# Turning the attention output by DMA during the forward chain instead of in the FFN phase and the gradient phase

## The chip, the core and the metric

The kernel runs on one core of a Trainium2 chip. The metric is the device time of one execution in microseconds (us); the time before is the median of three runs. Matmuls run on TensorE (PE, with its weight loads on PEld), copies out of PSUM and elementwise work on VectorE (DVE) and ScalarE (ACT), some copies on GpSimd (POOL). DMAs are issued from two places: SyncE's queue (SP; plain copies and transposing copies) and POOL's queue (plain copies). Both kinds are carried out by the same 16 DMA engines.

## The reference, cut to what matters

A forward pass and its gradient for one layer: pre-LN attention with a recurrent memory, then a SwiGLU FFN. 2048 tokens of width 448, 16 heads of 256 (so the concatenated heads O have 4096 columns), 64 segments of 32 tokens with 8 memory tokens each.

```python
for s in range(n_seg):                       # 64 segments, each needs the memory of the one before
    h = concat([mem, xs])                    # 8 + 32 tokens
    q, k, v = h @ Wq, h @ Wk, h @ Wv         # 16 heads of 256
    p = softmax(mask(q @ k.T * scale))
    o = (p @ v) @ Wo                         # p @ v is O, 4096 columns
    mem = o[:, :M]; outs.append(o[:, M:])
h = x + attention(layernorm(x)); out = h + (silu(g) * u) @ w_down   # g, u from layernorm(h)
# and the gradients of x, mem0, Wq, Wk, Wv, Wo, w_gate, w_up, w_down
```

The gradient of Wo is the product of O, transposed, with the gradient of the attention's output, summed over all tokens. For that, O is needed with tokens on the partitions. The forward chain leaves it with columns on the partitions.

## The kernel before, in words

The order of all work is written by hand; each engine works through its own list in that order. There are four stages.

**Forward chain** (`forward_chain`, the loop from L785): 64 steps `s`, four to a tile of 128 tokens (`t, r = divmod(s, 4)`). A step projects K, Q and V (L818 to L844, matmuls L558 and L566), transposes K and Q (L572), computes the scores (L603), the softmax (L851 to L867), the transposed probabilities (L876), O (L910, in four groups: half 0 and half 1, each for two groups of heads), and O times Wo (L687), whose sum over partitions (L611, L616) is the memory that the next step starts with. Beside that, each step carries a quarter of the work on the memory rows of the neighbouring tile (`cur`, `late`, `late2`).

The V rows that L910 reads stand in one buffer, `V_sb` (one copy). It is filled from two sides. Rows 32 to 39 of each group of heads, the last tokens of the segment, come by four small DMAs from SP at the start of a step (`v_b_rows`, L751); the buffer must have been read by the step before, and at r = 0 the copy that the rows come from must have been made. The other rows come from `Vev` by `v_shift`: some by POOL, DVE and ACT copies, and three by DMAs from SP (`D_`, L755): half 0 of groups 2 and 3 as soon as ACT has copied the first half of V out of PSUM, half 1 of group 0 after the second half. L910's first group needs neither of the first two; the second needs them; the third needs the last one.

SP's list in a step is, in this order: `v_b_rows` (4 DMAs, L751), `v_shift` (3 DMAs, L755), the stores of K and Q (L858, L859), two stores of `V_sb` (L894), at r = 0 a load of the next tile's rows (L536), at r = 2 a store of the finished rows (L741). POOL's list: two small copies (L807, L808), two `v_shift` copies (L524), the store of the probabilities (L891), a small copy (L950), at two of four steps a store of K or Q of the next tile's last tokens (L663), and at r = 3 the stores of the tile's O: `OTA` (1 MB, L959) and `OTB` (256 KB, L960).

**FFN phase** (`ffn_phase`, the loop from L1256): 14 iterations `i` and an end written out. Iteration `i` runs the gate and up products of one tile, the gradients of the tile before, and stores z, the two FFN gradients and the gradient of h from POOL. A transposing DMA on SP turns z (L1280). After that, from i = 3 to i = 13, `o_turn(3)` (L1281, L1215) takes the next three pieces of O, from a list `quarters` of columns 0 to 2047 of all tiles: a transposing DMA from `OTA` to one of three buffers in the weights' region (L1220, SP, [128 x 1024] in eight blocks), and a store from there to `OTok` (L1221, POOL). In the last iteration and after it, Wv, Wk and Wq are loaded transposed for the backward chain, each in two pieces (`load_back`, L1034, SP), as the FFN weights that they overwrite are used up: the first half of Wv follows the last gate product (L1105). In between SP issues the first loads for the backward chain (L1501, L1503, L1511). The end's stores go through POOL: L1171, L1174, L1192, L1195.

**Backward chain** (`backward_chain`): 64 steps, last to first. The change does not touch it.

**Gradient phase** (`tail_phase`): 22 phases; phase `p` multiplies one loaded operand X of [128 x 16 or 20 tiles x 1024], and issues the load for phase p + 2 (`load_phase`). Phases 6 to 21 are the four quarters of the gradients of Wv, Wk, Wq and Wo, in the order of the list `seg`. A quarter is loaded turned, by 16 transposing DMAs on SP, one for each tile (`seg_x`, L1828), or plainly from `OTok`, by two DMAs (`seg_o`, L1836). Before the change the quarters 0 and 1 of Wo are loaded plainly and 2 and 3 turned.

The tiles of a stage lie at fixed places of one arena; the strings `FWD`, `FFN`, `BWD` and `TAIL` (L94 to L117) list names, sizes and places in bytes.

Of the kernel before, what the change touches and what calls it, by code (L numbers as in the profile page):

```python
# [10 lines left out]
BF16 = mybir.dt.bfloat16  # L11
# [4 lines left out]
P = 128  # L16
# [77 lines left out]
FWD = """oA#0:8192 oB#0:2048 bev:2048x2  # L94
kB#0:2048 qB#0:2048 bevv#0:2048 kB#1:2048 qB#1:2048 bevv#1:2048 PT0:1280 PT1:1280 P_sb0:1024 hB#0:256
xload:1024 aT#0:1024
kT:2560 qT:2560 Kev:2048 Qev:2048 E_sb:1280
@43264 oA#1:8192 oB#1:2048
@54016 V_sb:4096 hA:2048
@61184 part:2048 partB:2048 Vev:2048 aT#1:1024  # L100
xtmp:1024x2 x2load:1024x2 P_sb1:1024 S_sb:640x2 maskr:640 maskf:160 hB#1:256"""
FFN = """WdT:14336
h_ld:896x3 hn:1024x3 dout_ld#2:1024x2 dh_t:1792 lnb_prod:1792 lnb_t1:1792 dh_b:896 o_t:896x2
@30464 dout_ld#0:1024x2
# [389 lines left out]
def forward_chain(k: _K, hA, NWIN, Wq_sb, Wk_sb, Wv_sb, Wo_sb, maskr, work, stage, ff, feed):  # L494
    nc, tc = k.nc, k.tc
    S, D, M, H, Dh, HD = k.S, k.D, k.M, k.H, k.Dh, k.HD
    SEG, L, NSEG, NT, KC, DP, MC, DC = k.SEG, k.L, k.NSEG, k.NT, k.KC, k.DP, k.MC, k.DC
    X2 = k.aps["A_x"][0]
    ident, identf, dr = k.ident, k.identf, k.dr
# [254 lines left out]
    def D_(out, in_):  # L754
        nc.sync.dma_start(out=out, in_=in_)  # L755

    def v_shift(V_sb, Vev, half, gs, eng):
        for g in gs:
            gg, g2 = divmod(g, 2)
            o = V_sb[QB * gg:QB * gg + SEG, g2 * GF + half * HB:g2 * GF + (half + 1) * HB]  # L760
            eng(o, Vev[32 * g:32 * g + 32, half * HB:(half + 1) * HB])
# [23 lines left out]
    for s in range(NSEG):  # L785
        t, r = divmod(s, 4)
# [18 lines left out]
        kT = work.tile([P, MC, L], BF16, name="kT", bufs=1)  # L805
        qT = work.tile([P, MC, L], BF16, name="qT", bufs=1)
# [8 lines left out]
        Kev = work.tile([P, GF], BF16, name="Kev", bufs=1)  # L815
        Qev = work.tile([P, GF], BF16, name="Qev", bufs=1)
# [29 lines left out]
        mx, ssum, rs, S_sb = [], [], [], []  # L846
        E_sb = work.tile([P, 2, HQ, L], FP32, name="E_sb", bufs=1)
# [30 lines left out]
        def p_ev(half, e, eng):  # L878
            eng(PT[QB * e:QB * e + L, half, :, e * L:(e + 1) * L].rearrange("p (g a) n -> p g a n", g=2),
                ppt[half][QB * e:QB * e + L, 0:2 * P].rearrange("p (a g n) -> p g a n", a=2, g=2)[:, :, :, 0:L])  # L880
# [8 lines left out]
        p_ev(1, 0, V)  # L889
        p_ev(1, 1, V)  # L890
        nc.gpsimd.dma_start(out=dr["P_all"][s], in_=P_sb[0:NR].rearrange("p h n -> p (h n)"))  # L891

        for gg in range(2):
            nc.sync.dma_start(out=dr["Vtok"][s, gg], in_=V_sb[QB * gg:QB * gg + 48, :])  # L894
        if s == NSEG - 3:
            next(feed)

# [29 lines left out]
        for i in range(MC):  # L927
            c = order[i]
# [95 lines left out]
def load_back(k, v, src, head, c0=0, c1=None):  # L1024
    nc = k.nc
    D, HD = k.D, k.HD
    if head:
        full = D // P
        for kc in range(full):
            nc.sync.dma_start_transpose(out=v[:, kc, :], in_=src[:, kc * P:(kc + 1) * P])  # L1030
        nc.sync.dma_start_transpose(out=v[:, full, :], in_=src[:, D - P:D])
        nc.gpsimd.memset(v[0:P - (D - full * P), full, :], 0.0)
    else:
        nc.sync.dma_start_transpose(out=v[:, c0:c1, :], in_=src[:, c0 * P:c1 * P])  # L1034


def ffn_phase(k: _K, WT, ff, work, mv2, rstd2, srcs, back):
    nc, tc = k.nc, k.tc
    S, D, F = k.S, k.D, k.F
    NT, KC, DP, FC = k.NT, k.KC, k.DP, k.FC  # L1040
    ps1, ident, dr = k.ps1, k.ident, k.dr
# [24 lines left out]
    def load(t):  # L1066
        o = T[t]
        o.h = work.tile([P, D], BF16, name="h_ld", bufs=3)
        nc.sync.dma_start(out=o.h[:], in_=dr["Hh"][rows(t), :])
        o.dout = work.tile([P, DP], BF16, name="dout_ld", bufs=4)  # L1070
        nc.sync.dma_start(out=o.dout[:, 0:D], in_=GO2[rows(t), :])
        nc.sync.dma_start(out=o.dout[:, D:DP], in_=GO2[rows(t), D - rem:D])
# [65 lines left out]
    def turn_f(src, dst, engs):  # L1138
        for half in range(2):
            pzb = ps1(BF16)  # L1140
            for j in range(FH):
                c = half * FH + j
                nc.tensor.transpose(pzb[:, j * P:(j + 1) * P], src[:, c * P:(c + 1) * P], ident[:, :])
            engs[half](dst[:, half * FH:(half + 1) * FH, :], pzb[:, 0:FH * P].rearrange("p (c n) -> p c n", n=P))

    def dz(t):
        o = T[t]
        o.dz = work.tile([P, F], BF16, name="dz", bufs=1)
        for pair in range(NB // 2):
            for b, pz in enumerate(mm_d(o.doutT, ff.WdT, pair)):  # L1150
                f = slice((2 * pair + b) * BW, (2 * pair + b + 1) * BW)
                A(o.dz[:, f], pz[:, 0:BW])

    def down_mm(t):
        T[t].pf = k.fix[0]
        for c in range(FC):
            nc.tensor.matmul(T[t].pf[:, 0:D], lhsT=ff.zT[:, c, :], rhs=ff.Wd[:, c, :], start=(c == 0), stop=(c == FC - 1))
# [30 lines left out]
    def dh_ln(t):  # L1188
        o = T[t]
        dh_t = work.tile([P, D], FP32, name="dh_t", bufs=1)  # L1190
        k.ln_bwd(dh_t[:], k.fix[1][:, 0:D], o.hn[:, 0:D], rstd2[:, t:t + 1], o.dout[:, 0:D], work, smal, D)
        nc.gpsimd.dma_start(out=dr["DH"][rows(t), :], in_=dh_t[:])  # L1192
        o.dhb = work.tile([P, D], BF16, name="dh_b", bufs=1)
        V(o.dhb[:], dh_t[:])
        nc.gpsimd.dma_start(out=dr["DHb"][rows(t), :], in_=o.dhb[:])  # L1195
# [14 lines left out]
        A(dT[:], pt[:, 0:KC * P])  # L1210
        nc.gpsimd.dma_start(out=dr["doutT"][t], in_=dT[:])

    quarters = [(t, q) for t in range(NT) for q in range(2)]

    def o_turn(n):  # L1215
        for t, q in quarters[:n]:
            b = ff.ot[len(quarters) % 3]
            del quarters[0]
            cols = slice(q * 1024, (q + 1) * 1024)
            nc.sync.dma_start_transpose(out=b.rearrange("n (c p) -> n c p", p=P), in_=dr["OTA"][t][:, cols])  # L1220
            nc.gpsimd.dma_start(out=dr["OTok"][t][:, cols], in_=b)  # L1221
# [34 lines left out]
    for i in range(NT - 2):  # L1256
        t, n1, n2 = ORD[i:i + 3]
        if i > 0:
            load(n2)
        if i == 2:  # L1260
            load_back(k, WT["o"], srcs["o"], True)
        if i == NT - 6:
            next(back)
        if not 1 < i < NT - 2:
            turn_f(T[t].z, ff.zT, (A, A))
        dz(t)
        if i > 0:
            dh_ln(t - 1)
        down_mm(t)
        if i == 0:  # L1270
            rstd(NT - 1, NT)
        grads(t)
        if i > 0:
            dh_out(t - 1)
        gate(n1)
        down_ev(t)
        norm(n2)
        up(n1)
        if 0 < i < NT - 3:
            nc.sync.dma_start_transpose(out=ff.zT, in_=T[n1].z)  # L1280
        if 2 < i < NT - 2:  # L1281
            o_turn(3)
        if i == NT - 3:
            dout_turn(n1)
            hn_turn(n2)
            gate(n2)
            load_back(k, WT["v"], srcs["v"], False, 0, HC)
            up(n2)
            load_back(k, WT["v"], srcs["v"], False, HC, 2 * HC)
            dh_turn(t)  # L1290
            slope(n1)
            slope(n2)
        else:
            dh_turn(t)
            dout_turn(n1)
            hn_turn(n2)
            slope(n1)
        dh_mm(t)
    p, q = ORD[NT - 2:]
# [483 lines left out]
def tail_phase(k: _K, work):  # L1783
    nc, tc = k.nc, k.tc
    S, D, M, HD, F = k.S, k.D, k.M, k.HD, k.F
    SEG, NSEG, NT, KC, MC = k.SEG, k.NSEG, k.NT, k.KC, k.MC
    ps1, ident, identf, dr = k.ps1, k.ident, k.identf, k.dr
# [37 lines left out]
    def seg_x(srcA, q, p):  # L1825
        X = k.Wall[:, k.xpos[p] * 512:k.xpos[p] * 512 + NKT * 1024].rearrange("p (t f) -> p t f", t=NKT)
        for t in range(NT):
            nc.sync.dma_start_transpose(out=X[:, t, :].rearrange("n (c p) -> n c p", p=P),  # L1828
                                        in_=srcA[t][:, q * 1024:(q + 1) * 1024])
        return X  # L1830

    def seg_o(q, p):
        X = k.Wall[:, k.xpos[p] * 512:k.xpos[p] * 512 + NKT * 1024].rearrange("p (t f) -> p t f", t=NKT)
        v = dr["OTok"].rearrange("t n f -> n t f")[:, :, q * 1024:(q + 1) * 1024]
        for a in range(0, NT, NT // 2):
            nc.sync.dma_start(out=X[:, a:a + NT // 2, :], in_=v[:, a:a + NT // 2, :])  # L1836
        return X
# [124 lines left out]
    Xs = {}  # L1962
    lds = {}
    lns = {}
    turned = [(w, q) for w in "vkq" for q in range(NQ)]
    seg = turned[0:3] + [("o", 0)] + turned[3:7] + [("o", 1)] + turned[7:12] + [("o", 2), ("o", 3)]
    assert NQ == 4
    srcA = {"v": dr["dVA"], "k": dr["dKA"], "q": dr["dQA"], "o": dr["OTA"]}
    srcB = {"v": dr["dVB"], "k": dr["dKB"], "q": dr["dQB"], "o": dr["OTB"]}
# [5 lines left out]
    def load_phase(p):  # L1975
        if p >= NP:
            return
        if p == 0:
            Xs[p] = (k.z_low, z_high)
        elif p < 6:  # L1980
            Xs[p] = k.ffn_half(ffn[p], p, 1)
        else:
            w, q = seg[p - 6]
            Xs[p] = seg_o(q, p) if w == "o" and q < 2 else seg_x(srcA[w], q, p)

    z_high = work.tile([P, NT // 2, F // 2], BF16, name="z_high", tag="h1")
    nc.sync.dma_start(out=z_high, in_=k.z_high)
# [6 lines left out]
    for p in range(NP):  # L1994
# [23 lines left out]
        if 5 <= p < NP - 1:  # L2018
            if p not in lds:
                w, q = seg[p - 5]  # L2020
# [14 lines left out]
        else:  # L2035
            w, q = seg[p - 6]
# [45 lines left out]
```

## Time and profile before

| | us |
|---|---|
| median of three runs | 2923.17 (2922.85 to 2923.99) |
| the profiled execution, its own time | 2936.97 |
| its span | 2935.2 |
| PE busy | 2722.7 (93% of the span) |
| DVE busy | 1561.3 |
| ACT busy | 1082.5 |
| POOL busy | 762.1 |
| from 60 to 950 us (forward chain): PE busy, DMA share | 847.10 of 890, 0.42 |
| from 2300 to 2910 us (gradient phase): PE busy, DMA share | 608.10 of 610, 1.04 |

The DMA share is the mean busy share of the 16 DMA engines; packets of two queues that overlap count twice, so it can pass 1. Time to landing of a DMA is shown for POOL's DMAs only. What is drawn for SP's DMAs is the time that SP takes to issue them, not the transfer. A releaser named "issue" is a wait for which the profile shows nothing.

### The profile page before, as it was taken

To read this page: it belongs to the slowest core of one execution; us is meant where nothing else is said; L and a number is where in the kernel's file an instruction comes from. 1 tells how busy PE (TensorE), PEld (TensorE's weight loads), DVE (VectorE), ACT (ScalarE), POOL (GpSimd) and SP (SyncE) were. 2 spreads that over 40 slices of the span, in tenths; PEclk is the share of its full clock that TensorE was granted. 3 is DMA by queue.
4 is the path that set the end of the run, shared out by engine and by line. 5 is a ranking of instruction groups with operands and counts; after the bars stand their busy time and mean duration, and the time that the engine had idled before them with its cause. 6 is when DMAs were issued, how large, how long until landed. Compare 5 with 4: busy or idle time off the path is not lost.

```text
span 2935.2 us, 104407 instructions
## 1 busy us (share of the span) xinstructions
PE 2722.7 (93%) x44384; PEld 1514.8 (52%) x44420; DVE 1561.3 (53%) x4196; ACT 1082.5 (37%) x2880; POOL 762.1 (26%) x1420
## 2 busy tenths in 40 slices
PE   3999999999998799987999999999999999999999
PEld 1555555555554455543555555555555454545454
DVE  4666666666665578874666666666665112222221
ACT  2444444444443455552444444434433111111110
POOL 2222222222222223321222222222222222233222
PEclk7999999999999899998999999999999999999999
DMA  9334434343435899997655655565556999999992
GB/s 273 116 123 134 126 123 137 116 130 122 135 116 140 217 218 233 245 226 166 151 156 153 189 152 161 155 175 152 161 151 215 334 228 227 209 225 241 204 224 69
DMA packets 652001, 515.86 MB, mean 176 GB/s; under 512 B 508592, under 2 KB 558112, under 8 KB 642000
## 3 DMA queue, kind: packets, MB, share of 16 engines
q1 hardware_dynamic: 600640, 309.09, 47.5%
q0 software_dynamic: 50896, 200.09, 20.5%
q8 instruction: 350, 5.73, 0.8%
q14 instruction: 115, 0.94, 0.1%
HBM read 145.89 MB, written 230.33 MB: 128 GB/s over the span
## 4 chain that ended last, share of the span: by engine, by line
PE 69%; DVE 15%; DMA 7%; issue 5%; SPq 2%; ACT 2%; POOL 1%; DVEq 0%; ACTq 0%; POOLq 0%
PE psf L1919 13%; PE psf L558 9%; PE psf L1392 9%; DVE arena L1355 5%; PE psf L687 4%; PE psf L1880 4%; PE psf L1105 3%; PE psf L1701 3%; PE psf L566 3%; PE psf L1364 2%; PE psh L572 2%; PE psf L1932 2%; PE psf L910 2%; PE psf L1399 2%; DMA wall<-in_A_Wv_dram 2%
## 5 line engine op out<-in xcount | busy, mean ns | idle before, releaser
L1919 PE MATMUL psf<-wall,arena 128*128 128x512 bf16 (+1 forms) x1788 | 390.6, 373 | 1.9
L521 ACT CAST arena<-psf 128x512 bf16<-128x512 f32 (+2 forms) x560 | 235.8, 453 | 362.4 <-PE psf L558 251.3
L1392 PE MATMUL psf<-wall,arena 128*32 128x448 bf16 x6144 | 336.8, 361 | 17.0 <-DMA wall<-in_A_Wq_dram 11.9
L1358 ACT CAST arena<-psf 128x256 bf16<-128x256 f32 (+1 forms) x597 | 233.0, 417 | 304.2 <-PE psf L1364 214.0
L558 PE MATMUL psf<-wall,arena 112*32 112x512 bf16 x5120 | 308.9, 384 | 31.0 <-DMA wall<-in_A_Wk_dram 14.0
L1919 PEld LDWEIGHTS <-arena 128*128 128x128 bf16 x1824 | 176.2, 98 | 198.3 <-issue 4.7
L1807 DVE CAST arena<-psf 128x448 bf16<-128x448 f32 (+1 forms) x83 | 54.7, 659 | 418.7 <-PE psf L1919 267.1
L518 DVE CAST arena<-psf 128x512 bf16<-128x512 f32 (+2 forms) x432 | 191.8, 469 | 123.7 <-PE psf L558 83.8
L1392 PEld LDWEIGHTS <-arena 128*32 128x32 bf16 x6144 | 154.9, 98 | 135.7 <-issue 30.7
L558 PEld LDWEIGHTS <-arena 112*32 112x32 bf16 x5120 | 126.4, 97 | 161.8 <-issue 28.2
L1355 DVE CAST arena<-psf 128x256 bf16<-128x256 f32 (+1 forms) x339 | 164.8, 486 | 83.0 <-PE psf L1701 41.8
L1805 ACT CAST arena<-psf 128x512 bf16<-128x512 f32 (+1 forms) x75 | 42.2, 563 | 427.9 <-PE psf L1919 267.0
L566 PE MATMUL psf<-wall,arena 112*32 112x512 bf16 x2560 | 169.2, 385 | 9.4 <-DMA wall<-in_A_Wv_dram 9.4
L1364 PE MATMUL psf<-wall,arena 128*32 128x512 bf16 x2560 | 156.6, 381 | 1.2 <-DVE arena L1404 1.2
L521 ACT COPY arena<-psh 40x160 bf16<-40x160 bf16 (+2 forms) x320 | 119.2, 400 | 94.6 <-PE psh L670 52.8
L1752 POOL COPY arena<-arena 128x32 bf16<-128x32 bf16 x63 | 13.2, 210 | 541.5 <-DVE arena L1404 541.5
L1701 PE MATMUL psf<-arena 40*128 40x40 bf16 x6144 | 146.9, 178 | 3.2 <-issue 1.8
L687 PE MATMUL psf<-wall,arena 128*32 128x224 bf16 x5120 | 147.6, 265 | 1.1 <-issue 1.1
L524 POOL COPY arena<-arena 32x512 bf16<-32x512 bf16 x129 | 77.8, 603 | 267.9 <-ACT arena L521 264.2
L1701 PEld LDWEIGHTS <-arena 40*128 40x128 bf16 x6144 | 125.8, 93 | 33.8 <-issue 16.2
L1355 DVE COPY arena<-arena 32x512 bf16<-32x512 bf16 x384 | 133.8, 349 | 8.8
L1355 DVE COPY arena<-psf 128x192 f32<-128x192 f32 x64 | 22.9, 358 | 215.2 <-ACT arena L1358 215.2
(223 smaller groups left out, 4475.5 us busy)
## 6 DMA issues: line engine op xcount, KB each, us to landing
Vtok<-arena SPq DMA_DIRECT2D x128, 192.0 KB
KtokA<-arena SPq DMA_DIRECT2D x64, 256.0 KB
QtokA<-arena SPq DMA_DIRECT2D x64, 256.0 KB
OTA<-arena POOLq DMA_DIRECT2D x16, 1024.0 KB, 5.2
arena<-QtokA SPq DMA_DIRECT2D x128, 128.0 KB
arena<-KtokA SPq DMA_DIRECT2D x128, 128.0 KB
dVA<-arena POOLq DMA_DIRECT2D x16, 1024.0 KB, 5.2
dKA<-arena POOLq DMA_DIRECT2D x16, 1024.0 KB, 7.2
```

Source lines behind the costliest of these rows:

```text
L518: nc.vector.tensor_copy(out=out, in_=in_)
L521: nc.scalar.copy(out=out, in_=in_)
L558: nc.tensor.matmul(ps[32 * g:32 * g + 32, :], lhsT=stat(kc), rhs=W_sb[0:DB, kc, c0:c0 + HB], start=(kc == 0), stop=(kc == KC - 1))
L566: nc.tensor.matmul(ps[32 * g:32 * g + 32, :].rearrange("t (y d) -> t y d", y=2), lhsT=stat(kc), rhs=wv[:, x, :, half, e, :], start=(kc == ...
L687: nc.tensor.matmul(ps[32 * g:32 * g + 32, 0:2 * DB], lhsT=x, rhs=Wo_sb[:, c, a * 2 * DB:(a + 1) * 2 * DB], start=first, stop=last)
L1355: nc.vector.tensor_copy(out=out, in_=in_)
L1358: nc.scalar.copy(out=out, in_=in_)
L1364: nc.tensor.matmul(ps[32 * g:32 * g + 32, :], lhsT=stat(kc), rhs=WoT_sb[:, kc, c0:c0 + HB], start=(kc == 0), stop=(kc == KC - 1))
L1392: nc.tensor.matmul(pO[32 * g:32 * g + 32, 0:D], lhsT=ch(c), rhs=WT[:, c, :], start=(first and i < 4), stop=(last and i >= MC - 4), skip_gr ...
L1701: nc.tensor.matmul(po[:, n * L:(n + 1) * L], lhsT=lhs[b:b + L, lc:lc + P], rhs=rhs[b:b + L, hh, 0:L], start=True, stop=True)
L1880: nc.tensor.matmul(ps[:, 0:D], lhsT=stat[:, i, c * P:(c + 1) * P], rhs=Y[:, i, 0:D], start=(i == 0), stop=(i == kts - 1))
L1919: nc.tensor.matmul(ps[:, 0:N], lhsT=Hx[:, i, dc * P:(dc + 1) * P], rhs=X[:, i, b * N:(b + 1) * N], start=(i == 0), stop=(i == kts - 1))
```

## The change

The 64 pieces of O (16 tiles, four quarters of 1024 columns) are all turned once and stored to `OTok`: 57 in the forward chain, one in each step from s = 4 to s = 60, for the tile in front (`o_turn(t - 1, r)`, after the stores of `V_sb`), and seven in the FFN phase, one in each iteration from i = 3 to i = 9. In the forward chain the store from the turned piece to `OTok` (`o_store`) stands one step later on POOL, behind the store of the probabilities, just ahead of the next turn. All turned pieces of the forward chain share one buffer, `oturn`, of 2 KB a partition, for which a small tile (`hB#1`) moves. In the gradient phase all four quarters of Wo are loaded plainly, and stand at every fourth place of the list. The number of PE, DVE and ACT instructions stays the same.

```diff
-kT:2560 qT:2560 Kev:2048 Qev:2048 E_sb:1280
+kT:2560 qT:2560 Kev:2048 Qev:2048 E_sb:1280 hB#1:256
...
-xtmp:1024x2 x2load:1024x2 P_sb1:1024 S_sb:640x2 maskr:640 maskf:160 hB#1:256"""
+xtmp:1024x2 x2load:1024x2 P_sb1:1024 S_sb:640x2 maskr:640 maskf:160
+@75776 oturn:2048"""
...
+    turned = []
+
+    def o_store():
+        for t, q, b in turned:
+            nc.gpsimd.dma_start(out=dr["OTok"][t][:, q * 1024:(q + 1) * 1024], in_=b)
+        turned.clear()
+
+    def o_turn(t, q):
+        b = work.tile([P, 1024], BF16, name="oturn", bufs=1)
+        nc.sync.dma_start_transpose(out=b.rearrange("n (c p) -> n c p", p=P), in_=dr["OTA"][t][:, q * 1024:(q + 1) * 1024])
+        turned.append((t, q, b))
...
         nc.gpsimd.dma_start(out=dr["P_all"][s], in_=P_sb[0:NR].rearrange("p h n -> p (h n)"))
+        o_store()
 
         for gg in range(2):
             nc.sync.dma_start(out=dr["Vtok"][s, gg], in_=V_sb[QB * gg:QB * gg + 48, :])
+        if 0 < t and s < NSEG - 3:
+            o_turn(t - 1, r)
...
-    quarters = [(t, q) for t in range(NT) for q in range(2)]
+    quarters = [(NT - 2, q) for q in range(1, 4)] + [(NT - 1, q) for q in range(4)]
...
-        if 2 < i < NT - 2:
-            o_turn(3)
+        if 2 < i:
+            o_turn(1)
...
-    seg = turned[0:3] + [("o", 0)] + turned[3:7] + [("o", 1)] + turned[7:12] + [("o", 2), ("o", 3)]
+    seg = turned[0:3] + [("o", 0)] + turned[3:6] + [("o", 1)] + turned[6:9] + [("o", 2)] + turned[9:12] + [("o", 3)]
...
-            Xs[p] = seg_o(q, p) if w == "o" and q < 2 else seg_x(srcA[w], q, p)
+            Xs[p] = seg_o(q, p) if w == "o" else seg_x(srcA[w], q, p)
```

More of the change, by code (lines that the diff above doesn't have):

```diff
@@ L96 @@
 xload:1024 aT#0:1024
-kT:2560 qT:2560 Kev:2048 Qev:2048 E_sb:1280
+kT:2560 qT:2560 Kev:2048 Qev:2048 E_sb:1280 hB#1:256
 @43264 oA#1:8192 oB#1:2048
@@ L100 @@
 @61184 part:2048 partB:2048 Vev:2048 aT#1:1024
-xtmp:1024x2 x2load:1024x2 P_sb1:1024 S_sb:640x2 maskr:640 maskf:160 hB#1:256"""
+xtmp:1024x2 x2load:1024x2 P_sb1:1024 S_sb:640x2 maskr:640 maskf:160
+@75776 oturn:2048"""
 FFN = """WdT:14336
```

## The prediction

> **What bounds the kernel now.** I read the windows first, one for each stage. Columns: length, then busy time and instructions of PE, PEld, DVE, ACT and POOL, granted clock, DMA share, GB/s.
>
> ```profile
> span 2935.2 us, 104407 instructions
> ```
> ```profile
> 60.00:950.00 890.00, 847.10 (x17522) 491.21 (x17514) 571.32 (x1798) 423.33 (x1063) 212.23 (x454) 0.99 0.42 128
> 1083.00:1102.00 19.00, 19.00 (x133) 10.11 (x132) 15.59 (x28) 10.63 (x19) 6.22 (x13) 1.00 0.99 243
> 1197.00:1216.00 19.00, 18.78 (x131) 9.82 (x130) 15.66 (x27) 10.43 (x20) 5.34 (x10) 1.00 1.15 253
> 1260.00:1265.00 5.00, 3.87 (x22) 1.71 (x22) 2.71 (x6) 2.98 (x7) 1.07 (x2) 1.00 1.06 349
> 1335.00:1340.00 5.00, 0.03 (x4) 0.02 (x7) 0.00 (x0) 0.00 (x0) 0.00 (x0) 0.50 1.17 266
> 2300.00:2910.00 610.00, 608.10 (x3635) 310.84 (x3670) 120.68 (x227) 76.50 (x107) 180.97 (x251) 1.00 1.04 219
> ```
>
> Three of the four places that the change touches are told by these rows. In the gradient phase PE is busy 608.10 of 610 us: its DMAs are loaded to the brim, but they hide. In the body of the FFN phase (1083 to 1102) PE is busy all 19 us, with the DMA engines at 0.99. At the end of the FFN phase (1335 to 1340) PE stands still for 5 us and the DMA engines do not: there transfers set the time. In the forward chain PE is busy 95% and the DMA engines only 42%.
>
> Next, the chain of waits of one forward step (r = 1), start and length:
>
> ```profile
> 410.14 3.64 PE psf L558 x64
> ...
> 419.50 0.48 PE psf L910 x8
> ...
> 423.89 3.64 PE psf L558 x64
> ```
>
> A step takes 13.75 us, and no DMA stands in its chain. In a few steps one does: the `v_shift` DMA that fills `V_sb` before L910. The first row is from such a step, the second from the waits:
>
> ```profile
> 388.02 3.64 DMA arena<-arena
> ```
> ```profile
> PE psf L910 <- DMA arena<-arena: 13.4, 14, 6.0
> ```
>
> So L910 has little cover against a late DMA. That is where the change can cost.
>
> **Forward chain: 57 turns and 57 stores added.** The price of a turn, from the FFN phase and from the backward chain (SP's issue time in ns), the time to landing of L1221's stores, and the DMA engines' time on SP's queue in the 12 us from 1244:
>
> ```profile
> L1220 SPq DMA_TRANSPOSE wall<-OTA x32: 1259/1998/3070, 1075.0 to 1256.9; - x32
> ```
> ```profile
> L1511 SPq DMA_TRANSPOSE arena<-Vtok x128: 1229/1293/2972, 1195.4 to 2220.1; - x128
> ```
> ```profile
> DMA to landing us min/median/max: 2.4/3.1/7.8
> ```
> ```profile
> q1 hardware_dynamic: 5181, 1.43, 81.7%
> ```
>
> In that window 1.43 MB, nearly all of it turns, took 0.817 x 12 = 9.8 us of all 16 engines: 0.262 MB is 1.8 us. SP issues a turn in 1.3 us where the queue is quiet and in 2.0 to 3.1 where it is full. The store of 256 KB at the 373 GB/s of the row below is 0.7 us. Together 2.5 us of DMA in a step of 13.75 that now has 0.42 x 13.75 = 5.8. Room there is; the question is where it lies:
>
> ```profile
> 398.00:400.00 2.00, 2.00 (x42) 0.84 (x31) 0.83 (x2) 0.59 (x1) 1.36 (x4) 1.00 0.97 373
> 400.00:402.00 2.00, 2.00 (x33) 1.17 (x34) 1.18 (x3) 1.12 (x2) 0.00 (x0) 1.00 0.95 312
> 402.00:404.00 2.00, 2.00 (x72) 1.53 (x72) 1.42 (x5) 1.10 (x3) 1.15 (x2) 1.00 0.21 73
> 414.00:416.00 2.00, 2.00 (x42) 1.17 (x40) 1.18 (x3) 1.01 (x3) 0.00 (x0) 1.00 0.04 8
> ```
>
> Now SP's and POOL's lists around two step borders, r = 3 to 0 at 396.35 and r = 1 to 2 at 423.89:
>
> ```profile
> 392.11 0.85 SPq L894 DMA_DIRECT2D Vtok<-arena  x2
> 397.30 4.38 SPq L751 DMA_DIRECT2D arena<-arena  x4
> 402.76 2.50 SPq L755 DMA_DIRECT2D arena<-arena  x3
> ...
> 420.34 0.85 SPq L894 DMA_DIRECT2D Vtok<-arena  x2
> 424.10 2.73 SPq L751 DMA_DIRECT2D arena<-arena  x4
> 430.30 2.40 SPq L755 DMA_DIRECT2D arena<-arena  x3
> ```
> ```profile
> 390.95 0.55 POOL L891 DMA_DIRECT2D P_all<-arena  x1 [1.63 <-DVE arena L867]
> 396.97 0.58 POOL L959 DMA_DIRECT2D OTA<-arena  x1 [0.34 <-ACT arena L521]
> ...
> 419.48 0.55 POOL L891 DMA_DIRECT2D P_all<-arena  x1 [1.62 <-DVE arena L867]
> ```
> ```profile
> SPq L751 <- DMA Vtok<-arena: 72.8, 38, 4.0
> ```
>
> There is one `oturn`, so the turn waits on SP until the store of the piece before, issued just ahead of it, has landed. That is a new wait. Behind it on SP stand the loads and stores of L536 and L741, `v_b_rows` and `v_shift`; for these L910 waits. Border at 423.89: POOL issues the store at 419.48 + 0.55 = 420.03; by the median it lands at 423.1; the turn is issued by 424.4; `v_b_rows`, which now start at 424.10 because the stores of `V_sb` land then (the 38 waits above), take 2.73 and end at 427.1. `v_shift` is due at 430.30: 3.2 us of cover remain, and the turn's 1.8 us on the engines fall into the quiet ahead of it (0.04 at 414 to 416, the same place one step earlier). At 396.35: store issued 391.50, landed 394.6, turn out by 395.9, before `v_b_rows` may start at 397.30. They end at 401.68, 1.1 us ahead of `v_shift` at 402.76. Here the engines are full with `OTA` from 398 to 402; a turn that started at 396 is through or nearly so, and what is left of it, up to 1.8 us, delays `v_shift`. There are 14 such steps (s = 8 to 60): 0 to 25 us. I take 0.3 us each, 14 x 0.3 = **4 us**, near the lower end, because the turn is issued 2 us before the stores start. The other 43 steps I take at 0.
>
> Both ends for the wait: at the least (landing 2.4, issue 1.23) it hides everywhere, 0. At the most (7.8 and 3.07) the turn at 420.03 is out at 430.9, `v_b_rows` at 433.6, `v_shift` 3.3 us late in every step: 57 x 3.3 = 188 us. The row nearest to this place is the median of 3.1, with the engines at 0.42 rather than the 0.99 where it was measured, so I stay near the low end. Nothing makes the chain shorter. POOL's extra 0.55 us a step lies in an idle stretch (its next DMA is at 396.97).
>
> **FFN phase: 25 turns and 25 stores fewer.** In the body PE is full: 0. In one iteration a turn of z came late because four turns for the backward chain stood ahead of it; its PE cost is the row below, of which I take 0.4 back (bounds 0 and 0.7). At the end:
>
> ```profile
> PEld L1157 <- DMA wall<-wall: 0.7, 1, 0.7
> ```
> ```profile
> 1261.13 5.89 PE L1105 MATMUL psf<-wall 128*128 128x448 bf16 x32 [1.40 <-ACT wall L1056]
> ```
> ```profile
> 1255.49 4.38 SPq L1220 DMA_TRANSPOSE wall<-OTA  x2
> 1264.20 28.18 SPq L1034 DMA_TRANSPOSE wall<-in_A_Wv_dram  x2
> ```
> ```profile
> 1262.03 0.54 POOL L1221 DMA_DIRECT2D OTok<-wall  x1
> 1265.20 0.54 POOL L1221 DMA_DIRECT2D OTok<-wall  x1 [2.63 <-DMA wall<-OTA]
> ```
> ```profile
> PE psf L1392 <- DMA wall<-in_A_Wq_dram: 11.9, 2, 7.0
> ```
>
> From 1264.2 until Wq has landed near 1340 the DMA engines never rest, and PE waits 11.9 us for Wq. This chain of loads starts when the gate product that begins at 1261.13 has read its weights, so turns that landed before 1264 cannot shorten it; they only leave the engines free earlier. What lies beyond 1264.2 and goes: the end of the last turn (0.4) and two stores of 0.26 MB, at 349 GB/s 1.5 us. Together **2.0 us**. Bounds: 0, and all five turns and five stores from 1244 on, 5 x (1.8 + 0.7) = 12.5.
>
> **Gradient phase: 32 turns fewer, two plain quarters more.**
>
> ```profile
> 2491.89 28.90 SPq L1828 DMA_TRANSPOSE wall<-dVA  x12
> ```
>
> Twelve turns took 28.9 us of SP, so sixteen take longer than a phase of 32.7 us, but PE lost only 1.9 of 610 us. Reordering keeps PE's work the same. I take 0; bounds 0 and 1.9.
>
> **The sum** against the profiled execution (2936.97 us; 1.8 of it around the span of 2935.2): +4 - 0.4 - 2.0 - 0 = +1.6. The median lies 13.8 us (0.5%) below the profiled time; differences this small carry over: 2923.2 + 1.6 = **2924.8**.
>
> **The rivals.** (B) SP's list is late.
>
> ```profile
> L755 SPq DMA_DIRECT2D arena<-arena x189: 507/536/1572, 66.5 to 944.1; - x189
> ```
>
> If the store lands halfway between median and maximum (5.45 us) and the turn issues in 3.07, as in the full queue of the FFN phase, `v_b_rows` end at 420.03 + 5.45 + 3.07 + 2.73 = 431.3, 1.0 late, and at the border to r = 0 at 391.5 + 8.52 + 4.38 = 404.4, 1.6 late. About 0.8 of that is free, since the last of the three `v_shift` DMAs waits for ACT (three of 0.54 us spread over 2.40). It decides once the turn is out more than 4.5 us after the next step began, or 2.8 at r = 0. Price: 14 x 0.8 + 43 x 0.5 (0.2 as worked, more where `v_b_rows` take 4.4) = 33 us, so 2954. For it: 38 waits already show DMAs landing late at this place. Against: the 3.2 us of cover.
>
> (C) The DMA engines take the turn and the `OTA` store together, and `v_shift` queues behind: 14 x 1.8 = 25, less 2.4: 2946. For it: the z turn above, late behind four others. Against: it starts 2 us ahead of the stores. The Trainium skill, "DMA: Bandwidth & Descriptors", section "Queues, rings and completion order", says that an engine consumes one queue's descriptors in ring order and shares itself between queues packet by packet, which speaks for this case; the late z turn agrees with it (0.7 us of PE), but no row here separates order from load.
>
> (D) The end of the FFN phase gains the whole 12.5 us: +4 - 0.4 - 12.5 = -8.9: 2914. For it: the engines are at 0.99 there. Against: the start at 1264.2 is PE's.
>
> That the change does not do what it says can be ruled out: 57 + 7 = 64 pieces.
>
> **How the numbers follow.** Forecast 0.53, B 0.22, C 0.13, D 0.12. About 0.2% (5.8 us) is what a measurement of this kernel can tell from no change. Of the forecast 0.43 lie within it, 0.07 above (its 14 steps at 1 us) and 0.03 below; B and C are slower, D faster: slower 0.42, same 0.43, faster 0.15. The range takes in C, most of D and the lower half of B: 2913 to 2955. The forecast's own range is 2919 to 2934.
>
> **What would show it.** Right: L1220's counterpart on SP starts about 3 us after the stores of `V_sb`, `v_shift` still starts 6.4 us after its step, steps stay at 13.75 with r = 0 slightly longer, Wq lands some 2 us earlier against the start of Wv, the gradient phase keeps its length. B would show as `v_shift` after 6.4 us in all steps, C as L910 waiting for DMAs at r = 0 alone, D as a much shorter wait at L1392. I am wrong if stores land later than 6 us, or if the gradient phase moves.

## The result, and the profile after

| | before | after |
|---|---|---|
| median, us | 2923.99 (5 runs, 2922.85 to 2935.56) | 2952.08 (5 runs, 2942.94 to 2956.38) |
| after / before, 95% interval | | 1.0066 (1.0043 to 1.009) |
| the profiled execution, us | 2936.97 | 2954.37 |

The change makes the kernel slower by 0.7%. That is about 19 us; the medians lie further apart because the runs before fall into two groups, near 2923 and near 2935, and their median takes one of them.

First the span of the kernel after from its page, then its windows, for the same stages as those shown of before (columns as there):

```profile
span 2952.5 us, 104467 instructions
```
```profile
60.00:960.00 900.00, 849.97 (x17377) 491.37 (x17374) 567.91 (x1788) 421.09 (x1057) 241.23 (x506) 0.98 0.58 157
1102.00:1121.00 19.00, 19.00 (x133) 10.11 (x132) 15.65 (x27) 10.63 (x19) 4.85 (x9) 1.00 0.73 177
2310.00:2920.00 610.00, 604.93 (x3617) 308.54 (x3651) 120.44 (x227) 76.50 (x107) 181.75 (x252) 1.00 1.02 222
```

The turns have moved as intended: the forward chain's DMA share rises from 0.42 to 0.58, that of the FFN iteration falls from 0.99 to 0.73, and PE is as full there as it was. The price is in the first row: 900 us hold 17377 PE instructions where 890 us of before held 17522.

The stages, cut in all three traces at the same instructions (us). "Again" is a second trace of before (run before_again), so the columns before and again show how far one kernel differs between two executions.

| stage | before | again | after |
|---|---|---|---|
| forward, start of step 3 to start of step 60 | 795.8 | 795.8 | 819.2 |
| start of step 60 to the FFN phase's first product of dh (the gradient of h) | 110.8 | 108.2 | 114.3 |
| FFN, first to 13th such product | 232.4 | 235.0 | 232.6 |
| from there to the third backward step | 122.7 | 113.6 | 116.2 |
| backward chain | 888.7 | 884.2 | 886.6 |
| gradient phase | 656.2 | 656.1 | 661.2 |

Only the forward chain is far outside what before differs from itself. By step, means over s = 5 to 60, in us from the start of the step (period; when `v_b_rows` have been issued; when `v_shift` begins to be issued; when the last L910 group, L926 after, begins):

| r | before | after |
|---|---|---|
| 0 | 14.15; 5.40; 6.41; 10.59 | 15.30; 6.58; 6.85; 11.56 |
| 1 | 13.97; 3.50; 6.42; 10.56 | 14.30; 4.88; 6.61; 10.78 |
| 2 | 13.97; 3.15; 6.41; 10.55 | 13.98; 4.97; 6.45; 10.56 |
| 3 | 13.95; 4.59; 6.41; 10.54 | 14.20; 6.18; 6.61; 10.68 |

14 x (1.15 + 0.33 + 0.01 + 0.25) = 24 us, 16 of them at r = 0. One such step shows how: s = 28, which starts at 451.65 and takes 19.01 us. SP's list, then POOL's, from the timeline of after:

```profile
448.34 1.08 SPq L908 DMA_DIRECT2D Vtok<-arena  x2
453.12 3.73 SPq L767 DMA_TRANSPOSE arena<-OTA  x1
457.01 3.33 SPq L752 DMA_DIRECT2D arena<-arena  x4
460.45 2.42 SPq L756 DMA_DIRECT2D arena<-arena  x3
```
```profile
447.24 0.56 POOL L904 DMA_DIRECT2D P_all<-arena  x1 [1.62 <-DVE arena L880]
447.79 0.57 POOL L762 DMA_DIRECT2D OTok<-arena  x1
452.26 0.54 POOL L975 DMA_DIRECT2D OTA<-arena  x1 [0.32 <-ACT arena L522]
452.79 0.54 POOL L976 DMA_DIRECT2D OTB<-arena  x1
```

The store of the piece before is issued at 447.79. SP is free at 449.4, but the turn leaves only at 453.12, 5.3 us after the store. By then POOL has issued the 1.25 MB of `OTA` and `OTB`. Beside them the turn takes 3.73 us to issue, `v_b_rows` start at 457.01 instead of about a us after the step's start, and `v_shift` at 460.45, 8.8 us into the step instead of 6.4. PE, and its windows:

```profile
463.51 0.43 PE L926 MATMUL psf<-arena 104*128 104x80 bf16 x4 [2.50 <-DMA arena<-arena]
466.16 3.18 PE L688 MATMUL psf<-wall,arena 128*32 128x224 bf16 x64
```
```profile
457.00:462.00 5.00, 3.80 (x108) 2.30 (x100) 3.71 (x14) 2.92 (x7) 2.00 (x4) 1.00 0.78 117
462.00:464.00 2.00, 0.43 (x4) 0.27 (x4) 0.02 (x1) 0.00 (x0) 0.32 (x1) 0.61 0.73 233
464.00:466.00 2.00, 1.70 (x28) 1.20 (x28) 0.40 (x1) 0.37 (x1) 0.00 (x0) 0.50 0.98 325
466.00:468.00 2.00, 2.00 (x44) 1.60 (x45) 0.69 (x3) 0.85 (x4) 0.00 (x0) 0.50 0.64 166
468.00:470.00 2.00, 1.86 (x38) 1.24 (x26) 0.39 (x1) 0.26 (x2) 0.00 (x0) 0.68 0.55 108
```

L926 waits 2.5 us for `V_sb`, and then the granted clock is down to 0.50. (The description of the kernel before has it that the first group of this product needs neither of the first two `v_shift` DMAs. By the code it reads the columns of groups 0 and 2, so it needs the first of them, and here it is the first four matmuls that wait.) Four of the 14 steps at r = 0 (s = 28, 32, 36, 60: 19.01, 17.44, 16.66, 17.23) go this way. They are 70.3 - 4 x 14.15 = 13.7 us of the 16. Against the same four steps of before (60.3 us together) it is 10.1: s = 60 took 16.39 us there too, with the clock down to 0.50 for 3.41 us.

Over the whole forward chain, first SP's waits, then the turn's row, then what ended PE's idle time ahead of L926 (us, times):

```profile
SPq L767 <- DMA OTok<-arena: 173.0, 52, 4.7
```
```profile
L767 SPq DMA_TRANSPOSE arena<-OTA x57: 1262/1314/3726, 124.3 to 931.7; - x57
```
```profile
  DMA arena<-arena: 24.2, 32
  issue: 40.4, 67
```

In 52 of 57 steps the turn waits for the store. Ahead of L910 the first of the last two rows was 13.4 us in 14 times, and "issue" 21.6 in 31. Together that is 29.6 us more, though not all idle time lengthens a step.

### The profile page after: what moved, and what is told of

Its sections match the earlier page's. It is cut to its first block, busy times and chain, and to the rows that moved or that the text cites. A ratio compares the mean times of both kernels' runs of the same rounds, so it can differ in the third digit from the quotient of the medians.

```text
span 2952.5 us, 104467 instructions
## 1 busy us (share of the span) xinstructions
PE 2732.8 (93%) x44384; PEld 1518.7 (51%) x44420; DVE 1561.6 (53%) x4196; ACT 1082.4 (37%) x2880; POOL 782.7 (27%) x1452
## 4 chain that ended last, share of the span: by engine, by line
PE 68%; DVE 14%; DMA 7%; issue 6%; ACT 2%; POOL 2%; SPq 2%; DVEq 0%; ACTq 0%; POOLq 0%
PE psf L1935 12%; PE psf L559 9%; PE psf L1408 8%; DVE arena L1371 5%; PE psf L688 4%; PE psf L1121 4%; PE psf L1896 4%; PE psf L1717 3%; PE psf L567 3%; DMA arena<-arena 3%; PE psf L1380 3%; PE psh L573 2%; PE psf L1948 2%; PE s_ps L1201 2%; PE psf L926 2%
## 5 line engine op out<-in xcount | busy, mean ns | idle before, releaser
L688 PE MATMUL psf<-wall,arena 128*32 128x224 bf16 x5120 | 152.8, 271 | 0.0
```

The source lines that it names most:

```text
L688: nc.tensor.matmul(ps[32 * g:32 * g + 32, 0:2 * DB], lhsT=x, rhs=Wo_sb[:, c, a * 2 * DB:(a + 1) * 2 * DB], start=first, stop=last)
```

## The experiments

Three theories. **The wait** (W): the turn waits on SP for the store of the piece before, which is issued too late in the step; held up, the turn meets the `OTA` store and delays `v_b_rows` and `v_shift`. **The work itself** (R): 57 turns and stores cost their time in the forward chain wherever they are issued. **The reorder** (F): the rearranged FFN and gradient phases cost it. Forward lengths below are from step 3 to step 60. Without turns in the forward chain they were 795.8 to 803.9 in five traces, mean 799.6, so after's 819.2 is 19.6 more.

| kernel | ratio to before (95%) | forward, us | gradient phase, us |
|---|---|---|---|
| after | 1.0066 (1.0043 to 1.009) | 819.2 | 661.2 |
| forward_alone | 1.0108 (1.0061 to 1.0155) | 818.5 | 668.1 |
| rest_alone | 0.9968 (0.9947 to 0.9989) | 799.7 | 656.4 |
| store_first | 0.9969 (0.9946 to 0.9992) | 801.6 | 660.0 |
| store_first_again | 0.9964 (0.994 to 0.9988) | 801.7 | 671.4 |
| no_r3 | 1.0009 (0.9985 to 1.0034) | 799.8 | 658.4 |
| ota_later | 1.0218 (1.0179 to 1.0257) | 871.1 | 656.4 |
| ffn_alone | 0.9995 (0.9972 to 1.0017) | 802.9 | 657.8 |
| tail_alone | 0.9997 (0.9976 to 1.0017) | 803.9 | 657.4 |

**forward_alone**: before, with the forward chain's 57 turns and stores added and nothing taken away.

```diff
+        o_store()
...
+        if 0 < t and s < NSEG - 3:
+            o_turn(t - 1, r)
```

> The 57 turns and stores of the forward chain as in the change; the FFN phase (three turns an iteration) and the gradient phase (two quarters of Wo turned) as before, so 32 pieces of O are turned and stored twice. Theory W (the turn waits on SP until the store ahead of it has landed, 5.0 us by the median of the changed kernel's trace, and pushes the small DMAs of the next step back; worst at r = 0, where the store of the tile's O fills the queue): steps s = 4 to 60 together 20 to 28 us longer than before (24.3 in the changed kernel), FFN phase and gradient phase as before, 2923 + 24 = 2947 us. Rival F (part of the loss sits in the gradient phase, which was 5 us longer in the changed kernel, and does not come from the forward chain): the same 24 us here, and the gradient phase stays at its old length; then the reordered quarters are to blame for the 5 us.

The loss of the forward chain is all there, 818.5 - 799.6 = 18.9 us over the mean. From its waits on SP:

```profile
SPq L767 <- DMA OTok<-arena: 182.7, 53, 5.6
```

The old order of the gradient phase took 668.1 us in this execution, longer than after's 661.2. So F finds nothing to explain here. The ratio of 1.0108 is some 32 us, more than the forward chain's 18.9; its interval holds 1.0066, and where the rest lies is open.

**rest_alone**: after without the turns of the forward chain. The gradient phase reads those quarters from `OTA` instead.

```diff
-        if 0 < t and s < NSEG - 3:
-            o_turn(t - 1, r)
...
-        v = dr["OTok"].rearrange("t n f -> n t f")[:, :, q * 1024:(q + 1) * 1024]
+        v = dr["OTA"].rearrange("t n f -> n t f")[:, :, q * 1024:(q + 1) * 1024]
```

> The change without any turn in the forward chain: 57 pieces of O are not turned, and the plain loads of the gradient phase read the unturned O instead, in the same shape and size (so the gradient of Wo is computed from wrong data). It shows what the FFN phase and the gradient phase gain or lose by themselves. Theory W: forward steps as before; the end of the FFN phase 6.5 us shorter and one iteration 0.4 shorter, as in the changed kernel's trace; the gradient phase 0 to 5 us longer; 2923 - 7 + (0 to 5) = 2916 to 2921 us. Rival F: gradient phase 5 us longer as in the changed kernel, 2921. Rival (the 6.5 us are a chance of one execution and my 2.0 us were right): 2921 with the old length of the gradient phase.

The forward chain is back at 799.7, and the rest of the change is no loss: 0.3% faster than before. So F falls.

**store_first**: after, with the store that frees the buffer moved forward on POOL by some seven us (medians: 3.2 us into the step instead of 9.9): behind the two small copies at the start of the step, no longer behind the store of the probabilities. The turn stays where it is, and all the work is done.

```diff
         nc.gpsimd.tensor_copy(out=qT[:, :, SEG:L], in_=T.qB[:, :, r * M:(r + 1) * M])
+        o_store()
...
         nc.gpsimd.dma_start(out=dr["P_all"][s], in_=P_sb[0:NR].rearrange("p h n -> p (h n)"))
-        o_store()
```

> The change with one line moved: the store of the turned piece is issued by POOL right after its two copies at the start of the next step instead of behind the store of the probabilities, so it has landed long before the next turn, and the turn does not wait. All work is done. Theory W: the turn starts right after the stores of V_sb, 3 us before the next step begins, v_shift starts on time, and the 24 us of the forward chain fall to under 8: 2923 + 8 - 7 = about 2924 or less. Rival R (the turn's own 1.8 us of traffic ahead of the small DMAs in the same queue costs the time, not the wait): the turn starts early but the chain still loses 18 us or more, 2940 to 2950.

> The version with the store moved up, measured once more, beside the changed kernel's other variant and the kernel before. Theory W: faster than the kernel before by 0.2 to 0.5%, forward chain 4 to 8 us longer than before. If the first measurement was a chance: a ratio of 1.000 and more.

The store now comes right after the turn that fills the buffer, and the next turn some eight us after the store. SP's and POOL's lists at the same border, r = 3 to 0, in store_first (step 28 starts near 451.6), the idle time ahead of L926, and the time to landing of the store (L762; the second of these is forward_alone's):

```profile
448.24 0.94 SPq L908 DMA_DIRECT2D Vtok<-arena  x2
449.23 2.47 SPq L767 DMA_TRANSPOSE arena<-OTA  x1
452.64 4.41 SPq L752 DMA_DIRECT2D arena<-arena  x4
457.97 2.44 SPq L756 DMA_DIRECT2D arena<-arena  x3
```
```profile
440.89 0.54 POOL L762 DMA_DIRECT2D OTok<-arena  x1 [0.46 <-issue]
...
452.17 0.57 POOL L975 DMA_DIRECT2D OTA<-arena  x1 [0.32 <-ACT arena L522]
```
```profile
  DMA arena<-arena: 12.3, 18
```
```profile
DMA to landing us min/median/max: 2.3/2.6/5.9
```
```profile
DMA to landing us min/median/max: 2.8/5.3/7.3
```

The turn leaves right behind the stores of `V_sb` and is issued before the `OTA` store starts; `v_shift` begins 6.41 us into the step again. No wait of L767 for `OTok` is left in the view of SP's waits, and the idle time ahead of L926 is that of before. The store itself lands after 2.6 us instead of 5.3; it no longer goes out among those of K, Q, V and the probabilities. The turns, which now follow these at once, take longer to issue (median 2.34 us, 1.31 in after), and it costs nothing: they start 8.1 us behind the store and wait for nothing. Same turns, same stores, same bytes: 801.6 and 801.7 us, 2 above the mean. So W holds, and R is at most these 2 us, inside the spread of kernels without turns; by its ratio the version is as fast as rest_alone, which does none of the 57 turns. It is faster than both kernels, twice.

**no_r3**: after without the turns of r = 3, those that stand at the border to r = 0 (quarter 3 is then read from `OTA`).

```diff
-        if 0 < t and s < NSEG - 3:
+        if 0 < t and s < NSEG - 3 and r < 3:
...
-        v = dr["OTok"].rearrange("t n f -> n t f")[:, :, q * 1024:(q + 1) * 1024]
+        v = dr["OTA" if q == 3 else "OTok"].rearrange("t n f -> n t f")[:, :, q * 1024:(q + 1) * 1024]
```

> The change without the turns at r = 3 (quarter 3 of 14 tiles is not turned; its plain load in the gradient phase reads the unturned O, so that quarter of the gradient of Wo comes from wrong data). The r = 0 steps, which follow, held 15 of the 24 us. Theory W with the collision at r = 0 (the turn issued at r = 3 meets the store of the tile's O): the mean r = 0 step falls from 15.0 to about 14.0 us, the others stay, forward chain 24 - 15 = about 9 us longer than before. Rival R (every turn costs alike wherever it stands): the forward chain loses 43/57 of 24 = 18 us, and the gain is not in the r = 0 steps alone.

```profile
SPq L767 <- DMA OTok<-arena: 103.8, 28, 5.1
```

The remaining turns still wait, up to 5.1 us, and the forward chain is 799.8, with r = 0 at 14.04. In this trace a late turn costs about 0.1 us at the borders to r = 2 and 3, where no `OTA` store stands: what costs is the late turn at the one border with the big store. The times say it less sharply. This trace is of the second fastest of the ten executions (2929.91 us); their median, 2937.37, is 9.3 us above rest_alone's and 9.7 above store_first's, measured in the same series. What the other late turns cost in the executions that took longer isn't shown.

**ota_later**: after, with the `OTA` and `OTB` stores moved a few us back, behind the first `v_shift` copies of POOL. The wait stays, but the turn would no longer meet them.

```diff
         v_shift(V_sb, Vev, 0, (0, 1), G_)
+        ot_store()
...
-            nc.gpsimd.dma_start(out=dr["OTA"][t], in_=T.oA[:].rearrange("p c n -> p (c n)"))
-            nc.gpsimd.dma_start(out=dr["OTB"][t], in_=T.oB[:].rearrange("p c n -> p (c n)"))
+            done.append(T)
```

> The change, with the wait kept and the store of a finished tile's O (1 MB and 256 KB) moved from the start of the r = 0 step to 7.7 us after it, behind POOL's two v_shift copies. All work is done. Theory W (at r = 0 the late turn meets that store, so that it issues slowly and the small DMAs land late): the mean r = 0 step falls from 15.05 us to 14.4 or less, though the store now lies beside the last v_shift DMA. Rival (the late turn alone costs, by SP's list and its own 1.8 us on the engines, wherever the store is): r = 0 stays at 14.8 or more, and the r = 1 step is not better than 14.3.

This missed by far: r = 0 takes 18.83 us. At the border of step 28 (start 481.35), SP, POOL, then the chain that ended last:

```profile
482.72 1.89 SPq L774 DMA_TRANSPOSE arena<-OTA  x1
484.78 2.70 SPq L752 DMA_DIRECT2D arena<-arena  x4
487.76 2.40 SPq L756 DMA_DIRECT2D arena<-arena  x3
```
```profile
489.02 0.54 POOL L763 DMA_DIRECT2D OTA<-arena  x1
489.55 0.54 POOL L764 DMA_DIRECT2D OTB<-arena  x1
```
```profile
489.66 5.14 DMA arena<-arena
```

Half of the expectation came true: away from the big stores the late turn is issued in 1.89 us here (3.73 in after), and `v_shift` leaves on time, 6.41 us into the step. But now its last DMA leaves 0.6 us behind the `OTA` store, and its 32 KB take 5.14 us. The wait is not all that the step loses: in each of the 14 steps at r = 0 the granted clock falls too, to a mean over the step of 0.82 to 0.91 (0.82 in this one). So there are two ways to be late at r = 0, and both need the big store: SP's list is late when the turn must be issued beside it, and `v_shift` lands late when it is on the way beside it. In before the store is issued 5.8 us ahead of `v_shift` (396.97 and 402.76), and that place is the better one.

**ffn_alone** and **tail_alone**: before with only the FFN change, and before with only the new order and the plain loads of the gradient phase (what isn't turned by then is read from `OTA`).

```diff
-        if 2 < i < NT - 2:
-            o_turn(3)
+        if 2 < i:
+            o_turn(1)
```
```diff
-            Xs[p] = seg_o(q, p) if w == "o" and q < 2 else seg_x(srcA[w], q, p)
+            Xs[p] = seg_o(q, p) if w == "o" else seg_x(srcA[w], q, p)
```

> The kernel before with the change of the FFN phase alone: seven turned pieces instead of 32. Nothing is turned in the forward chain, and the gradient phase keeps its old order; its two plainly loaded quarters of Wo read the unturned O in the same shape and size (so half of the gradient of Wo comes from wrong data). The FFN phase and the gradient phase of the change together gave a ratio of 0.9968 (0.9947 to 0.9989). My prediction gave the FFN phase -2.4 us, which is a ratio of 0.9992; the theory that the FFN phase holds the whole gain gives 0.997.

> The kernel before with the change of the gradient phase alone: all four quarters of Wo loaded plainly, each after three turned ones; the quarters 2 and 3 read the unturned O (so half of the gradient of Wo comes from wrong data). Forward chain and FFN phase as before. My prediction gave this 0, a ratio of 1.000 (at most 1.9 us, 0.9994); the theory that the gradient phase holds the gain, because fewer turns spare it waits for late loads in some executions (its length differed from 656 to 671 us), gives 0.997 or 0.998.

Neither differs from before by more than its interval. Their intervals overlap with that of rest_alone too, so the 0.3% of rest_alone and store_first can't be shared out. One part is visible: the iteration in which four turns for the backward chain stand ahead of the z turn, here in tail_alone, which keeps the old FFN phase (SP, then PE):

```profile
1199.65 6.91 SPq L1511 DMA_TRANSPOSE arena<-Vtok  x4
1209.19 7.39 SPq L1280 DMA_TRANSPOSE wall<-wall  x1
1216.69 7.16 SPq L1220 DMA_TRANSPOSE wall<-OTA  x3
```
```profile
1222.21 5.34 PE L1157 MATMUL s_ps<-wall 128*128 128x448 bf16 x14 [5.12 <-DMA wall<-wall]
```

In the four traces with the old FFN phase that iteration took 19.2, 22.0, 20.0 and 26.6 us, in the seven with the new one 18.81 each time: 3.1 us on average.

**before_again**: before unchanged, one look, for the spread of the stages.

> The kernel before once more, for a second look at its stages: how far they differ between executions of the same kernel. If the gain at the end of the FFN phase is real (theory: fewer turns and stores ahead of the loads for the backward chain), the stretch from the last but two gradient product of the FFN phase to the third step of the backward chain stays near 120 to 123 us (116.2 in the changed kernel); if 122.7 was a chance, it lies near 117. The gradient phase was 656 to 668 us long in the kernels so far, with the old order and with the new one; if that is chance, it lies anywhere in that span here too.

2924.72 us; its stages stand beside those of before and after. It is why the 6.5 us that the FFN phase's end seems to gain in the first pair of traces (122.7 to 116.2) isn't put down to the change: before itself took 113.6.

## Why the prediction was off, point by point

The time lies in the range, but not where the forecast put it: 2952 against 2924.8, with a range of its own of 2919 to 2934. It lies in it because the range was stretched over the rivals B and C; that it comes near B's 2954 is luck, since B priced the wrong steps. The step that failed is "store issued 391.50, landed 394.6, turn out by 395.9", the forward chain's **+4**.

- **When the buffer comes free: wrong.** I took 3.1 us from the store's issue to the turn, the median of the FFN phase, and argued from the mean DMA share, 0.42 against 0.99, that it could only be less. Measured: a median of 5.0 us (2.9 to 5.9). The mean share said nothing about the two us in which the store is issued: by the sizes of the DMA view the same step's stores of K, Q, V and the probabilities (256 + 256 + 2 x 192 + 104 KB) are issued from 446.8 to 449.4, around the 256 KB of the piece. Moved away from them in store_first, the store lands after a median of 2.6 us: so its place in the step is what made it late, and that its company is the reason is the likely reading, not a separate test.
- **The issue of a turn**: right in a quiet queue (1.3 us predicted, median 1.31). At the border to r = 0, where I had the turn out before the `OTA` store, the two met: median 1.98, up to 3.73.
- **Where it costs: right.** The 14 steps at r = 0 were named; they carry 16 of 24 us. The size was not: 1.15 us a step, where 0.3 was taken and 1.8 allowed. Of the 1.15, 0.44 is `v_shift` issued late (6.41 to 6.85), 0.53 its slower landing (last group 10.59 to 11.56, less the 0.44), and 0.18 comes behind the last group. The clock has a part in the last two and was in none of the cases: from s = 5 to 60 it is at 0.50 for 6.8 us at s = 28 and for 3.41 us each at s = 32, 36, 49, 55 and 60, 23.9 us in all, against 3.41 in before. An estimate from these: half of the difference, (23.9 - 3.4) / 2 = 10 of the 24 us at most.
- **The other 43 steps at 0**: nearly; 14 x (0.33 + 0.01 + 0.25) = 8 us. The trace of no_r3 shows about 0.1 us a step for the wait at r = 2 and 3. Of the rest, two steps hold most: s = 49 and s = 55 with 16.47 and 16.65 us, 2.5 and 2.7 over the mean of before. That these two come from the turns isn't shown: steps as long stand in kernels without a turn in the forward chain (rest_alone, s = 45: 16.64; ffn_alone, s = 52: 16.66; tail_alone, s = 18: 16.52).
- **Rivals B and C: both in part.** B had the landing (5.45; measured 5.0) but not the place: it priced all 57 steps, and away from r = 0 `v_shift` is late by 0.04 to 0.20 us, not 0.5. C had the place and nearly the sum (25; measured 16 at r = 0), but what I held against it, that the turn "starts 2 us ahead of the stores", rested on the landing that B doubted: in ten of the 14 steps at r = 0 the turn leaves up to 1.0 us behind the start of the `OTA` store. In eight of these ten `v_shift` begins at 6.56 us or later, in the four others at 6.41. I had weighed them as separate cases; B's late store is what brings C about. The 33 and 25 us were sums of the right order: after's forward chain is 19.6 us over the mean.
- **The skill's rule behind C**: the Trainium skill, "DMA: Bandwidth & Descriptors", section "Queues, rings and completion order", has an engine share itself between queues packet by packet. On its own that would let a small DMA through beside a large one. In ota_later the 32 KB on SP's queue took 5.14 us, and landed at 494.80, 1.5 us after the `OTA` store on POOL's queue (issued at 489.02, 4.3 us to landing). The 32 KB were not let through early; no run here tells whether sharing by packets or another cause held them up.
- **FFN iteration, -0.4**: the right wait, sized from one execution in which it happened to be small. Over four traces it is 3.1 us (0.4 to 7.8). The "bounds 0 and 0.7" were those of one trace.
- **FFN end, -2.0**: not shown. The stretch took 110.9 to 122.7 us in kernels with the old FFN phase (mean 116.3) and 111.8 to 118.9 with the new one (mean 115.0). The 122.7 is the execution that the prediction read.
- **Rival D: no.** The first half of Wk waits on SP until POOL's store of a turned gradient (`doutT`, L1227) has landed, so a faster Wv brings nothing. Nor is the faster Wv shown to come from the change: against 28.18 us at 1264.20 in the trace that the prediction read, before_again, the same kernel, took 17.58. First that row, then after:

```profile
1265.14 17.58 SPq L1034 DMA_TRANSPOSE wall<-in_A_Wv_dram  x2
```
```profile
1287.38 15.81 SPq L1050 DMA_TRANSPOSE wall<-in_A_Wv_dram  x2
1311.72 8.91 SPq L1050 DMA_TRANSPOSE wall<-in_A_Wk_dram  x1
```
```profile
SPq L1050 <- DMA doutTd<-wall: 8.1, 1, 8.1
```
```profile
PE psf L1408 <- DMA wall<-in_A_Wq_dram: 9.3, 2, 6.2
```

Behind Wv SP stands for 8.5 us ahead of Wk, 8.1 of them for the store. It does so in before_again as well (6.6). PE waits 9.3 us for Wq where it waited 11.9, but 8.3 in before's second trace.

- **Gradient phase, 0: right as far as can be told.** PE's waits there, after:

```profile
PE psf L1935 <- DMA wall<-dKA: 1.9, 3, 1.4
```

The old order took 656.1 to 668.1 us, the new one 656.4 to 671.4. What makes the same kernel's phase differ by 11 us (store_first and store_first_again: 660.0 and 671.4) stays open.

Two buffers for the turned pieces, which should take the wait away with the store left in place, were not tried: the lists of the forward chain leave 1760 bytes of a partition free, and a second buffer needs 2048. Where the 0.3% gain of store_first lies beyond the 3.1 us of the FFN iteration (0.3% is 9 us) is open as well.

## What to carry to other kernels

A buffer that is filled and emptied by DMA is as good as the place of the store that frees it: put that store right behind the fill, not right ahead of the next fill, and look at what else is issued in the same two us, not at the mean load of the stage. A wait in an in-order queue costs little where it stands and much where it pushes its follower into a big transfer, so price it at the border with the big transfer first. Take a term that comes from one wait in one execution from several executions before it is trusted.

## What the runs showed of the hardware

- A 256 KB store issued among about 1 MB of other stores had landed, by the start of the turn that waits for it, after a median of 5.0 us (after; 5.3 to landing in forward_alone). In the FFN phase of before, at a mean DMA share of 0.99, it landed after 3.1, and in store_first, away from the other stores of its step, after 2.6. So the mean share doesn't tell it.
- A DMA of 32 KB from SBUF to SBUF took 5.14 us when it was issued 0.6 us behind 1.25 MB of stores in another queue. The r = 0 steps of ota_later took 18.83 us, against 14.15 in before, by such a wait and the fall of the clock behind it.
- PE idle for 2.5 us was followed by a granted clock of 0.50. From 462 to 470 the windows give (1 - 0.61) / 0.5 x 2 + 4 + (1 - 0.68) / 0.5 x 2 = 6.8 us of it; the 64 matmuls of L688 took 3.18 us in it, and 1.72 elsewhere:

```profile
481.44 1.72 PE L688 MATMUL psf<-wall,arena 128*32 128x224 bf16 x64
```

This row is from the timeline of after, in step 29.

The other stretches at 0.50 of after between s = 5 and 60 are 3.41 us long, and in other kernels a shorter wait was enough: in tail_alone, s = 13, the longest is 0.85 us. There PE was busy for 2.46 of the 3.41 us ahead. In before, at s = 36, it was busy for 1.79 of 3.40 us, with a wait of 1.59, and the clock stayed at 1.00:

```profile
247.72:251.13 3.41, 2.46 (x39) 1.10 (x36) 2.30 (x9) 2.29 (x6) 0.55 (x1) 1.00 0.38 120
251.13:254.54 3.41, 3.41 (x72) 2.53 (x68) 0.69 (x3) 0.60 (x3) 0.00 (x0) 0.50 0.67 201
```
```profile
571.00:574.40 3.40, 1.79 (x44) 1.12 (x43) 1.97 (x7) 1.56 (x4) 0.56 (x1) 1.00 0.45 151
574.40:577.80 3.40, 3.13 (x82) 2.39 (x82) 1.33 (x6) 1.52 (x8) 0.00 (x0) 1.00 0.54 165
```

So neither the length of one wait nor the busy share of such a stretch alone settles it, and no run here shows a threshold.
